# All attention in float32 on quarters of TensorE's array, causal half only, with the first weights decoded first

## The chip, the core and the metric

The kernel runs on one core of a Trainium2 chip. Its engines are TensorE (PE in the profile; PEld is its weight load), VectorE (DVE), ScalarE (ACT), GpSimd (POOL) and SyncE (SP), whose queue issues the transfers. The metric is device time in microseconds (us), lower is better.

## The reference

Decayed causal attention over batch 4, 8 heads, 768 positions, head size 64, then a feed-forward network (FFN) with a squared ReLU, on 3072 tokens of 512 features.

```python
for b in range(nb):                                   # blocks of 64 positions
    intra = einsum('bhic,bhjc->bhij', qb, kb) * Dmask     # lam**(i-j) where i >= j, else 0
    intra = einsum('bhij,bhjd->bhid', intra, vb)
    inter = einsum('bhid,bhde->bhie', qb * lam**(pos+1), kv_state)
    out[:, :, sl] = intra + inter
    kv_state = lam**64 * kv_state + einsum('bhsd,bhse->bhde', kb * lam**(63-pos), vb)
x = out as (tokens, heads * 64)
h = maximum(x @ w_in, 0)                              # w_in 512 x 2048, float64
return (h * h) @ w_out                                # w_out 2048 x 512, float64
```

q, k, v are float32, lam is one number per head; the weights arrive as float64.

## The kernel before

**Work units.** The kernel works on chunks of 128 positions, all eight heads; there are 24 chunks (4 batches of 6). Three chunks make a tile of 384 tokens, and there are 8 tiles. For each tile the attention writes x, transposed, as two parts: `xh`, rounded to the type float32r, and `xl`, the rest. The FFN runs over 16 feature blocks `f` of 128. One *step* is one tile and one `f`: 12 matmuls into `h` (L514: xh with the high weights `wih`, xl with `wih`, xh with the low weights `wil`), the squared ReLU split into `gh` and `gl` on ScalarE and VectorE (L528 to L535), and 9 matmuls (L520, L521, L523) that add to three output banks. There are 128 steps. From the third tile on, two steps are taken together. A full tile's output is copied out (L569) and stored (L570).

**Weights.** For each `f` there are two weight blocks, `w_in` and `w_out`. Each is loaded as 64-bit words into `st` (L277) and decoded to float32 in `m`: one operation on ScalarE (L278), four on VectorE (L279, L281, L283, L285). Then ScalarE rounds it to the high part (L287) and VectorE subtracts for the low part (L288). The blocks stay on the chip, and tiles 0 and 1 run through `f` as the weights come.

**Attention.** Each chunk is done in two units of four heads. With the decay taken apart, the scores are masked (not decayed), v is weighted by a table `wdec`, and the output is multiplied by a table `rdec`; the state of a batch and head is kept, multiplied by `lc` from chunk to chunk. The 12 units of the two first tiles and 4 of the third (the 8 chunks of `PLAIN`) are `unit_plain`: float32 matmuls, scores with 64 rows of the array per head (L318), state and values (L372, L375), the update of the state (L346). The other 16 chunks (32 units) are `unit_split`: q, k, v, the masked scores and the state are each cast to a high part and a low part (`ab`, `ka`, `vv`, `pp`, `ss`), and float32r matmuls over the full array take high and low parts together (scores L436, state L478, values L479); VectorE and ScalarE cast, subtract and add the parts (L412 to L497). Only the update (L456) is float32. Scores are computed for the full 128 x 128 square and then masked.

**What sets the order.** `Plan` holds all operations with an engine, a planned duration, a key, dependencies and buffers (`SLOTS` gives the number of each kind; `bank` is a PSUM bank). `Plan.order` places them one after another: on each engine, of those that can start within 0.05 us, the one with the lowest key. The result is one fixed order for each engine, and each engine then runs its instructions in that order. All loads are issued from SP's queue, which takes them in order, so a load that waits for its buffer holds back the loads behind it. Early in the program the plan puts in matmuls on zeros (`filler`, L240) where TensorE would have nothing to do. The buffers of `unit_split` take the place of those of the decoding and of `unit_plain` when these are done (`late`).

Of the kernel before, what the change touches and what calls it, by code (L numbers as in the profile page):

```python
# [9 lines left out]
F32 = mybir.dt.float32  # L10
# [16 lines left out]
NQ = NP // 2  # L27
PK = 1536
# [12 lines left out]
N_PLAIN = 8  # L41
PLAIN, SPLIT = CHUNKS[:N_PLAIN], CHUNKS[N_PLAIN:]
# [10 lines left out]
class Op:  # L53
    def __init__(self, eng, dur, key, fn, deps, bufs, after, lat, early):
        self.eng, self.dur, self.key, self.fn, self.deps, self.bufs, self.after, self.lat, self.early = (
            eng, dur, key, fn, deps, bufs, after, lat, early)
        self.start = self.end = None


class Plan:  # L60
    LAT = {"PE": 0.25, "ACT": 0.15, "DVE": 0.12, "POOL": 0.12, "SP": 2.0}
    PORT = ("DVE", "POOL")
# [7 lines left out]
    def op(self, eng, dur, key, fn, deps=(), bufs=(), after=(), lat=None, early=None):  # L70
        o = Op(eng, dur, key, fn, [d for d in deps if d is not None], list(bufs), [d for d in after if d is not None], lat or self.LAT[eng], early)
        for b in o.bufs:
            b.left += 1
        self.ops.append(o)
        return o

    def order(self, pe_slow, fill):
# [10 lines left out]
        done, filled, early = [], 0, sum(o.early is True for o in self.ops)  # L88
        while any(ready.values()):
            best = None  # L90
            for e, ops in ready.items():
                can = []
                for o in ops:
# [5 lines left out]
                    ok = o.early is not False or not early  # L99
# [15 lines left out]
            if o.eng == "PE" and t < fill:  # L115

                while free["PE"] + (long := FILL * (2.0 if free["PE"] < pe_slow else 1.0)) < t:
# [3 lines left out]
                    done.append(Op("PE", long, 0, lambda i=bank[1]: self.filler(i), [], [], [], 0, None))  # L121
# [16 lines left out]
            early -= o.early is True  # L138
# [14 lines left out]
EARLY = ("pnt", "diag0", "diag1", "st", "m")  # L153
LATE = ("pkt", "ab", "ka", "vv", "pp", "z", "zl", "ss0", "ss1")

FIRST, SLOW_STEP, LAG, BEGIN2, SECOND, STEP, PE_SLOW, FILL_END, FILL = 18.0, 6.5, 16, 9.0, 1.5, 4.8, 7.0, 45.0, 0.43
# [3 lines left out]
SPARE = 0.8  # L162

TWO, BOTH = 2, 9.0


@with_exitstack
def kernel(ctx: ExitStack, tc: tile.TileContext, pn, pk, lamx, w, out):
# [3 lines left out]
    phase = ExitStack()  # L172
    plan = Plan()
    for k, n in SLOTS.items():
# [4 lines left out]
        "bank": ([P, 512], F32), "h": ([P, 512], F32),  # L179
        "gh": ([P, N], F32R), "gl": ([P, N], F32R), "g": ([P, N], F32), "ob": ([P, DM], F32),  # L180
        "s1": ([P, 4, C], F32), "vd": ([P, 4, D], F32), "us": ([P, 2, D], F32), "xr": ([P, 2, C], F32),
        "st": ([P, DM], U64), "m": ([P, DM], F32), "pnt": ([P, 4, 2, P], F32), "diag0": ([P, 2, P], F32), "diag1": ([P, 2, P], F32),
        "pkt": ([P, PK], F32), "ab": ([P, 4, 2, C], F32R), "ka": ([P, 4, C], F32R), "vv": ([P, 4, 2, D], F32R),
        "pp": ([P, 4, 2, C], F32R), "z": ([P, 2, 2, C], F32), "zl": ([D, 2, 2, C], F32),
        "ss0": ([P, 2, 2, 2, D], F32R), "ss1": ([P, 2, 2, 2, D], F32R), "hold": ([P, 2, D], F32)}
# [6 lines left out]
    make(ps, ("bank", "h"))  # L192
    make(const, [k for k in SLOTS if k not in EARLY + LATE + ("bank", "h", "x")])

    tables = const.tile([P, 16], F32, name="tables")
    wdec, lc = tables[:, 0:H], tables[:, H:H + NP]
# [4 lines left out]
    flip, zero = tiles["g"][-1][:, 0:P], tiles["ob"][-1]  # L201
    lam, ej, ec = (tiles["g"][-1][:, P + 16 * i:P + 16 * i + n] for i, n in enumerate((H + NP, H, NP)))
    mask = const.tile([P, P], F32, name="mask")
# [4 lines left out]
    make(phase.enter_context(tc.tile_pool(name="early", bufs=1)), EARLY)  # L208

    def late():  # L210
        phase.close()
        make(ctx.enter_context(tc.tile_pool(name="late", bufs=1, reuse_waits="tile")), LATE)

        for k in ("ss0", "ss1"):
            for s in tiles[k]:
                nc.gpsimd.memset(s.bitcast(F32), 0.0)
# [4 lines left out]

    def start_tables():
        nc.sync.dma_start(out=lam, in_=lamx)
        nc.vector.memset(zero, 0.0)
        nc.gpsimd.iota(ej, pattern=[[0, H]], base=MID, channel_multiplier=-1, allow_small_or_imprecise_dtypes=True)
        nc.vector.memset(ec, float(C))

        nc.vector.memset(flip, 1.0)
        nc.vector.memset(mask, 1.0)
        nc.gpsimd.affine_select(out=flip, in_=flip, pattern=[[1, P]], compare_op=ALU.is_equal, fill=0.0, base=1 - P, channel_multiplier=1)  # L230
        nc.gpsimd.affine_select(out=mask, in_=mask, pattern=[[1, P]], compare_op=ALU.is_ge, fill=0.0, base=0, channel_multiplier=-1)

        for d in tiles["diag0"] + tiles["diag1"]:
            nc.gpsimd.memset(d, 0.0)

        nc.gpsimd.tensor_tensor(out=wdec, in0=lam[:, 0:H], in1=ej, op=ALU.pow)
        nc.gpsimd.tensor_tensor(out=lc, in0=lam[:, H:H + NP], in1=ec, op=ALU.pow)
# [6 lines left out]
    o_start = plan.op("POOL", 1.2, -99, start_tables, early=True)  # L244


    o_pow = plan.op("POOL", 3.0, -98, lambda: None, [o_start], early=True)
    wb, rps = Buf("m"), Buf("bank")

    def turned():  # L250
        for n in range(NP):
# [411 lines left out]
```

## Time and profile before

| | |
|---|---|
| time, median of 3 runs | 633.93 us (633.67 to 634.47) |
| span of the profiled execution, first to last instruction | 631.5 us (the page gives no other time of it; the median is 2.4 more) |
| TensorE busy | 624.0 us, 99% |
| VectorE, ScalarE, GpSimd busy | 476.5, 360.9, 5.9 us |
| transfers | 57.24 MB, mean 91 GB/s |
| instructions | 9583 |

A matmul's record includes the time in the array's pipeline, so records of matmuls overlap: what a matmul costs is read from the spacing of starts, not from its duration. In a row of the timeline stand the start, the time from the first start to the last end, the engine, the line, the operation, `out<-in`, the array shape (rows*columns), the streamed operand (partitions x columns) and, behind the x, the number of instructions. In a row of the windows stand the stretch, its length, then busy us and (x instructions) of PE, PEld, DVE, ACT and POOL, the granted clock of TensorE as a share of full speed, the share of the DMA engines that is busy, and GB/s.

### The profile page before, as it was taken

Reading aid. Unit: us, or ns where it says so; the run is one execution under the profiler, and the core shown is the slowest. Engines: PE = TensorE matmul, PEld = TensorE weight load, DVE = VectorE, ACT = ScalarE, POOL = GpSimd, SP = SyncE. Lnnn points to the kernel's source line nnn. Section 1 sums busy time; section 2 is a strip of 40 time slices with the busy share of each in tenths; the row PEclk is TensorE's granted clock in tenths of the full one; section 3 lists DMA queues with packets and bytes.
Section 4 is the critical chain, followed back from the end, with each engine's and each line's share of the span. In section 5 each row is a group of like instructions: output and inputs, shape, how many; then the busy total and the mean of one; then the engine's idle time right before and its main releaser. Section 6 shows DMA issues by size and latency. Waiting matters only on the chain.

```text
span 631.5 us, 9583 instructions
## 1 busy us (share of the span) xinstructions
PE 624.0 (99%) x3608; PEld 568.7 (90%) x3608; DVE 476.5 (75%) x1078; ACT 360.9 (57%) x841; POOL 5.9 (1%) x15
## 2 busy tenths in 40 slices
PE   9899999999999999999999999999999999999997
PEld 7798999888999999999999999999999999999996
DVE  5999999846767997598965999669994799733222
ACT  5887777656856574376744666455753657522221
POOL 2000000000000000000000000000000000000000
PEclk9999999999999999999999999999999999999999
DMA  8735556523221220321303222131210411000001
GB/s 299 269 106 186 176 173 195 200 81 121 101 81 52 70 101 0 102 101 50 101 1 102 100 70 81 51 101 50 101 51 0 150 51 51 1 32 20 0 1 50
DMA packets 15166, 57.24 MB, mean 91 GB/s; under 512 B 1808, under 2 KB 1808, under 8 KB 15120
## 3 DMA queue, kind: packets, MB, share of 16 engines
q1 hardware_dynamic: 15120, 56.64, 26.3%
q8 instruction: 28, 0.46, 0.3%
q14 instruction: 18, 0.15, 0.1%
HBM read 50.34 MB, written 6.29 MB: 90 GB/s over the span
## 4 chain that ended last, share of the span: by engine, by line
PE 96%; DVE 3%; ACT 1%; issue 0%
PE h L514 42%; PE bank L523 14%; PE bank L520 14%; PE bank L521 14%; PE bank L479 2%; PE bank L478 2%; PE bank L436 2%; PE bank L456 2%; PE bank L318 1%; PE bank L240 1%; PE bank L375 1%; DVE s L323 1%; ACT diag L362 0%; PE bank L372 0%; DVE xr L378 0%; PE bank L346 0%
## 5 line engine op out<-in xcount | busy, mean ns | idle before, releaser
L520 PE MATMUL bank<-woh,gh 128*128 128x512 f32 x384 | 150.3, 392 | 0.0
L521 PE MATMUL bank<-wol,gh 128*128 128x512 f32 x384 | 150.1, 391 | 0.0
L528 ACT ACTIVATE g<-h 128x384 f32<-128x384 f32 x128 | 62.8, 491 | 144.2 <-PE h L514 143.4
L514 PE MATMUL h<-xh,wih 128*128 128x384 f32 x512 | 111.9, 340 | 0.0
L514 PE MATMUL h<-xh,wil 128*128 128x384 f32 x512 | 109.6, 336 | 0.0
L514 PE MATMUL h<-xl,wih 128*128 128x384 f32 x512 | 109.6, 336 | 0.0
L534 DVE TENSOR_TENSOR g<-g 128x384 f32<-128x384 f32 x96 | 53.4, 556 | 68.2 <-ACT gh L533 68.1
L523 PE MATMUL bank<-woh,gl 128*128 128x512 f32 x384 | 100.6, 390 | 0.2 <-DVE gl L535 0.2
L514 PEld LDWEIGHTS h<-xh,wih 128*128 128x128 f32 x512 | 89.7, 188 | 5.2
L514 PEld LDWEIGHTS h<-xh,wil 128*128 128x128 f32 x512 | 90.6, 188 | 0.0
L514 PEld LDWEIGHTS h<-xl,wih 128*128 128x128 f32 x512 | 90.3, 188 | 0.0
L523 PEld LDWEIGHTS bank<-woh,gl 128*128 128x128 f32 x384 | 71.7, 188 | 15.0 <-DVE gl L535 0.4
L520 PEld LDWEIGHTS bank<-woh,gh 128*128 128x128 f32 x384 | 72.2, 188 | 13.2 <-issue 0.2
L521 PEld LDWEIGHTS bank<-wol,gh 128*128 128x128 f32 x384 | 72.2, 188 | 13.1
L535 DVE TENSOR_TENSOR gl<-g,gh 128x384 fp32r<-128x384 f32 x128 | 70.7, 553 | 6.6 <-ACT gh L531 3.5
L533 ACT ACTIVATE gh<-g 128x384 fp32r<-128x384 f32 x96 | 50.5, 526 | 31.8 <-PE bank L521 30.5
L486 DVE TENSOR_TENSOR z<-bank,z 128x256 f32<-128x256 f32 x64 | 27.0, 421 | 25.1 <-ACT z L485 25.0
L447 ACT CAST pp<-s 128x512 fp32r<-128x512 f32 x32 | 19.9, 622 | 24.5 <-DVE s L445 24.5
L479 PE MATMUL bank<-pp,vv 128*128 128x256 f32 x128 | 32.0, 283 | 0.0
L478 PE MATMUL bank<-ab,ss 128*128 128x256 f32 x128 | 31.8, 282 | 0.0
L491 DVE TENSOR_TENSOR xr<-z,zl 64x256 f32<-64x256 f32 x64 | 26.7, 417 | 2.7 <-ACT zl L487 1.0
L569 DVE COPY ob<-bank 128x512 f32<-128x512 f32 x15 | 10.3, 689 | 22.0 <-PE bank L523 21.6
(80 smaller groups left out, 792.0 us busy)
## 6 DMA issues: line engine op xcount, KB each, us to landing
pkt<-pk SPq DMA_DIRECT2D x32, 768.0 KB, 4.4
st<-w SPq DMA_DIRECT2D x32, 512.0 KB, 3.3
pnt<-pn SPq DMA_DIRECT2D x16, 512.0 KB, 4.9
out<-ob SPq DMA_DIRECT2D x23, 256.0 KB, 2.3
out<-z SPq DMA_DIRECT2D x1, 256.0 KB, 2.0
g<-lamx SPq DMA_DIRECT2D x1, 6.0 KB, 1.6
```

The source lines that it names most:

```text
L478: nc.tensor.matmul(y4[:, n], at(ss)[:, n, h].rearrange("p t d -> p (t d)"), at(ab)[:, i], start=n == 0, stop=False, skip_group_check=True)
L479: nc.tensor.matmul(y4[:, n], at(vv)[:, i].rearrange("p t d -> p (t d)"), at(pp)[:, i], start=False, stop=True, skip_group_check=True)
L486: zo.append(add("DVE", 0.36, 2, lambda h=h, part=part: nc.vector.tensor_tensor(out=at(z)[:, h], in0=part(0), in1=at(z)[:, h], op=ALU.add), ...
L491: nc.vector.tensor_tensor(out=at(xr)[half(h)], in0=at(z)[0:64, h], in1=at(zl)[:, h], op=ALU.add)
L514: nc.tensor.matmul(at(h)[:, 0:N], wt[:, cc, :], xt[:, cc, :], start=k == 0, stop=k == 3 * NCC - 1)
L520: nc.tensor.matmul(at(os_[j]), at(gh)[:, sl], woh[f], start=f == 0, stop=False)
L521: nc.tensor.matmul(at(os_[j]), at(gh)[:, sl], wol[f], start=False, stop=False)
L523: nc.tensor.matmul(at(os_[j]), at(gl)[:, sl], woh[f], start=False, stop=f == NF - 1)
L528: orr = plan.op("ACT", 0.45, key, lambda: nc.scalar.activation(at(g), at(h)[:, 0:N], AF.Relu), [o1], [h, g])
L533: ogh = plan.op("ACT", 0.47, key, lambda: nc.scalar.activation(at(gh), at(g), AF.Square), [orr], [g, gh])
L534: og = plan.op("DVE", 0.48, key, lambda: nc.vector.tensor_tensor(out=at(g), in0=at(g), in1=at(g), op=ALU.mult), [orr, ogh], [g])
L535: ogl = plan.op("DVE", 0.48, key, lambda: nc.vector.tensor_tensor(out=at(gl), in0=at(g), in1=at(gh), op=ALU.subtract), [og, ogh], [g, gh, gl])
```

## The change

All 24 chunks now take one path in float32, on whole chunks of eight heads, and `unit_split` with its casts is gone. The array is used as four quarters of 64 x 64. Keys are taken in two halves of 64 (`j`), and for the second half of the keys only the second half of the queries is computed (`C - j * TW` columns), so that scores and values leave out the quarter above the diagonal. The matmuls of four quarters stand in turn (`QUARTERS`), and those that share rows of the array write to one bank, the others to another.

The four first chunks (`unit_first`) multiply their scores by a table of mask times decay (`dm`), which is built at the start (`spread`, L252, L266, L268); their v needs no weighting for the values, and their output no `rdec`. The other chunks (`unit`) mask, and use `wdec` and `rdec` as before. From the third tile on, one operation on TensorE holds a chunk's scores (L344) and update (L350) and the state (L452) and values (L358) of the chunk before it (`turn_over`). The weighting of v is on ScalarE in the two first tiles (L368), on VectorE later. The plan's keys put the first `w_in` block ahead of the loads of q, k and v. All eight banks are of one kind now (`h` takes one of them, with a token `turn` so that at most two do), buffers `in` are shared by weights and attention, and nothing is exchanged late. The FFN's matmuls are the same (now L485, L491, L492, L494), the decode too (now L289 to L300).

```diff
-FIRST, ..., SECOND, ... = 18.0, ..., 1.5, ...
+FIRST, ..., SECOND, ... = 9.0, ..., 5.0, ...
+TW = C // 2
+SPAN = C + TW
+QUARTERS = ((0, 0), (1, 1), (0, 1), (1, 0))
+WEIGHTS0, WKEY1, WKEY2, KLATE, ULATE = -9.0, 7.0, 2.0, 6.0, 16.0
...
+    def scores(t, sc):
+        for e in range(2):
+            for j in range(2):
+                for r, v in QUARTERS:
+                    o_ = at(sc[r])[half(v), e * SPAN + j * C:e * SPAN + j * C + C - j * TW]
+                    nc.tensor.matmul(o_, k_(t, r, 2 * v + e, j), q_(t, r, 2 * v + e, j * TW), ...)
+    def update(kt, vd, u, col, start):
+        for e in range(2):
+            for j in range(2):
+                for v, r in QUARTERS:
+                    nc.tensor.matmul(
+                        at(u[v])[half(r), col + e * D:col + e * D + D], kt()[half(v), head(r, j, e)],
+                        heads(at(vd))[half(v), head(r, j, e)], ...)
+    def values(v_, s1, ys, start):
+        for r in range(R):
+            for j in range(2):
+                for v, e in QUARTERS:
+                    nc.tensor.matmul(
+                        at(ys[v])[half(e), (2 + r) * C + j * TW:(3 + r) * C], v_()[half(v), head(r, j, e)], at(s1[r])[half(v), e, j * C:j * C + C - j * TW], ...)
...
     # unit(), every chunk but the four first
+        def both():
+            for v in range(2):
+                for r, e in QUARTERS:
+                    nc.tensor.matmul(at(ys[r])[half(e), v * C:v * C + C], at(old)[half(r), 2 * v + e], q_(t, r, 2 * v + e), ...)
+            values(lambda: heads(at(vd)), s1, ys, False)
+        def back(o_y):
+            oc = [add("ACT", ..., nc.scalar.copy(x4(xr)[:, 2 * r:2 * r + 2], at(ys[r])[:, 0:2 * C]...)) for r in range(R)]
+            oa = [add("DVE", ..., nc.vector.tensor_tensor(out=by_v(x4(xr), v), in0=y_(ys, v), in1=by_v(x4(xr), v), op=ALU.add)) for v in range(2)]
+            xo = add("DVE", ..., nc.vector.tensor_tensor(out=x4(xr), in0=x4(xr), in1=rdec, op=ALU.mult))
+            oh = add("ACT", ..., nc.scalar.copy(at(x)[0][:, :, cs], x4(xr)))
+            ol = add("DVE", ..., nc.vector.tensor_tensor(out=at(x)[1][:, :, cs], in0=x4(xr), in1=at(x)[0][:, :, cs], op=ALU.subtract))
...
     # unit_first(), the four first chunks
+        so = [add("DVE", ..., nc.vector.tensor_tensor(out=at(s1[r]), in0=at(sc[r])..., in1=dm()[:, 2 * r:2 * r + 2], op=ALU.mult)) for r in range(R)]
...
-        ws.append((weights(f, 0, t - 7), weights(f, 1, t - 2)))
+        ws.append((weights(f, 0, t - WKEY1 if f else WEIGHTS0), weights(f, 1, t - WKEY2)))
...
+    def turn_over(u):
...
+        def run(before=pending[0][0]["values"].fn if pending else None):
+            if f:
+                f.fn()
+            if before:
+                before()
```

How the order moves is shown at three places. A row gives the line, the operation, `out<-in` (numbers are buffers), and the shape that is streamed; x is a count.

VectorE near the start. Before, the first operations are the weighted v (`vd`) and the masked scores (`s`) of units:

```order
L255 COPY m_181<-tables 128x512
L332 TENSOR_TENSOR vd_90<-pnt_170,tables 128x256
L323 TENSOR_TENSOR s_0_88<-bank_61,mask 128x2x128
L323 TENSOR_TENSOR s_0_88<-bank_62,mask 128x2x128
L323 TENSOR_TENSOR s_1_89<-bank_64,mask 128x2x128
L323 TENSOR_TENSOR s_1_89<-bank_65,mask 128x2x128
L332 TENSOR_TENSOR vd_90<-pnt_172,tables 128x256
L259 TENSOR_TENSOR rdec<-bank_61,g_77 128x512
```

Now the same place on VectorE holds the decode of the first weight block (`m_102` from `in_86`) and the decay table (`in_89`):

```order
L259 COPY m_101<-tables 128x512
L262 TENSOR_TENSOR tables<-tables,g_77 128x4
L291 TENSOR_SCALAR m_102<-m_102 128x512
L293 TENSOR_SCALAR m_102<-m_102 128x512
L295 SCALAR_TENSOR_TENSOR m_102<-in_86,m_102 128x512
L266 SCALAR_TENSOR_TENSOR in_89<-bank_61,tables,mask 128x128 x4
L297 SCALAR_TENSOR_TENSOR m_102<-in_86,m_102 128x512
L268 COPY in_89<-in_89 128x4x64
L391 TENSOR_TENSOR s_0_91<-bank_62,in_89 128x384
L391 TENSOR_TENSOR s_1_92<-bank_63,in_89 128x384
```

The first block's decode has moved ahead of all scores; before, it began behind those of the first units.

TensorE around the first step. Before, the scores (L318) of nine units, six of tile 0 and three of tile 1, stand ahead of the first FFN matmuls (L514), and what directly surrounds these is:

```order
L375 MATMUL bank_63<-s_1_89,vd_91 64x128 x4
L346 MATMUL bank_61<-vd_91,pnt_173 64x64 x4
L346 MATMUL bank_65<-vd_90,pnt_170 64x64 x4
L514 MATMUL h_67<-xh_96,wih_103 128x384 x4
L514 MATMUL h_67<-xl_97,wih_103 128x384 x4
L514 MATMUL h_67<-xh_96,wil_119 128x384 x4
L372 MATMUL bank_64<-pnt_170,diag_0_174 128x128 x2
```

Now, on the same engine, the first FFN matmuls (L485) stand between the scores and the values of tile 1's first chunk:

```order
L344 MATMUL bank_68<-in_87 64x64
L344 MATMUL bank_61<-in_87 64x64
L485 MATMUL bank_62<-xh_105,wih_112 128x384 x4
L485 MATMUL bank_62<-xl_106,wih_112 128x384 x4
L485 MATMUL bank_62<-xh_105,wil_128 128x384 x4
L358 MATMUL bank_63<-s_2_93,half_95 64x128
L358 MATMUL bank_64<-s_2_93,half_95 64x128
```

The step has moved ahead of most of tile 1's attention; three steps of tile 0, not one, now stand ahead of the first step of tile 1, and the updates of tile 0's chunks come behind their values.

TensorE in a later tile. Before, a unit's state and values (L478, L479) stand between steps, its scores and update elsewhere:

```order
L514 MATMUL h_68<-xh_96,wil_132 128x384 x4
L478 MATMUL bank_62<-ab_1554,ss_0_1561 128x256
L479 MATMUL bank_62<-pp_1557,vv_1556 128x256
L478 MATMUL bank_62<-ab_1554,ss_0_1561 128x256
L479 MATMUL bank_62<-pp_1557,vv_1556 128x256
L478 MATMUL bank_63<-ab_1554,ss_0_1561 128x256
L479 MATMUL bank_63<-pp_1557,vv_1556 128x256
L478 MATMUL bank_63<-ab_1554,ss_0_1561 128x256
L479 MATMUL bank_63<-pp_1557,vv_1556 128x256
L514 MATMUL h_67<-xh_96,wih_117 128x384 x4
```

Now a part of one chunk's stretch reads (the end of the update, the state, and the first values of the chunk before):

```order
L350 MATMUL bank_67<-half_99,in_89 64x64
L452 MATMUL bank_62<-in_87,hold_80 64x128
L452 MATMUL bank_61<-in_87,hold_80 64x128
L452 MATMUL bank_62<-in_87,hold_80 64x128
L452 MATMUL bank_61<-in_87,hold_80 64x128
L452 MATMUL bank_62<-in_87,hold_80 64x128
L452 MATMUL bank_61<-in_87,hold_80 64x128
L452 MATMUL bank_62<-in_87,hold_80 64x128
L452 MATMUL bank_61<-in_87,hold_80 64x128
L358 MATMUL bank_62<-s_0_91,half_96 64x128
L358 MATMUL bank_61<-s_0_91,half_96 64x128
```

The 16 scores, 16 update, 8 state and 16 value matmuls of a stretch stand in one piece, once a chunk, and move between two pairs of steps.

More of the change, by code (lines that the diff above doesn't have):

```diff
@@ L87, in order @@
         slots = {k: [(0.0, i) for i in range(n)] for k, n in self.slots.items()}
-        done, filled, early = [], 0, sum(o.early is True for o in self.ops)
+        done, filled = [], 0
         while any(ready.values()):
@@ L207 @@
     wol = [const.tile([P, DM], F32R, name=f"wol{f}") for f in range(NF)]
[L208 to L216, printed above, removed]
     def at(b):
         return tiles[b.kind][b.slot]
+    halves = [slice(h * TW, h * TW + TW) for h in range(2)]
     def start_tables():
@@ L308, in add, with unit_first @@
+    def unit_first(b, x, col, key):
+        t, tv, tk, vd, s1, sc, ys, u, new = (
+            Buf("in"), Buf("half"), Buf("half"), Buf("half"), [Buf("s1") for _ in range(R)], [Buf("bank") for _ in range(2)], [Buf("bank") for _ in range(2)],
+            [Buf("bank") for _ in range(2)], Buf("hold"))
         def add(eng, dur, dk, fn, deps, bufs, name=None):
-            o = plan.op(eng, dur, key + dk, fn, deps, bufs, early=True)
+            o = plan.op(eng, dur, key + dk, fn, deps, bufs)
             return in_turn(name, o) if name else o
-        load = add("SP", 1.7, -8, lambda: nc.sync.dma_start(out=at(t), in_=pn[PLAIN.index((b, c)), q]), [o_start, behind], [t], "load")
@@ L313, in unit_plain @@
-        sc = [Buf("bank"), Buf("bank")]
-        def scores():
-            for n in range(2):
-                for h in range(2):
-                    nc.tensor.matmul(at(sc[h])[:, n * C:n * C + C], at(t)[half(h), 0, n], at(t)[half(h), 1, n], start=True, stop=True)
-        o = add("PE", 0.66, 0, scores, [load], [t] + sc, "sc")
-        if (b, c, q) == (0, 0, 0):
-            o_turned.after.append(o)
-        so = [add("DVE", 0.36, 0, lambda h=h: nc.vector.tensor_tensor(
-            out=at(s1).rearrange("p (n h) i -> p n h i", h=2)[:, :, h], in0=at(sc[h])[:, 0:2 * C].rearrange("p (n i) -> p n i", n=2),
-            in1=mask.unsqueeze(1).broadcast_to([P, 2, C]), op=ALU.mult), [o], [sc[h], s1], f"s1{h}") for h in range(2)]
@@ L377, in unit_plain @@
-        o = add("PE", 1.25 if old else 0.8, 0.2, values, so + [o_vd] + ([old[1]] if old else []), [y, t, vd, s1, x] + ([old[0]] if old else []), "y")
-        o = add("DVE", 0.35, 0.2, lambda: nc.vector.tensor_tensor(
-            out=at(xr), in0=at(y)[:, 0:2 * C].rearrange("p (n i) -> p n i", n=2), in1=rdec[:, prs], op=ALU.mult), [o, o_rdec], [y, xr], "xr")
-        cs = slice(col, col + C)
-        oh = add("ACT", 0.33, 0.2, lambda: nc.scalar.copy(at(x)[0][:, prs, cs], at(xr)), [o], [xr, x])
@@ L502 @@
     last_mm, steps = {}, {}
     def ffn(ti, f, x, ready, wo, os_, key, held):
[L506 removed]
+        h, turn_, gh, gl, g = (Buf(k) for k in ("bank", "turn", "gh", "gl", "g"))
         last = ti == len(TILES) - 1 and f == NF - 1
@@ new lines, with attention @@
+            if ti < 2:
+                done_x[ti] += unit_first(b, xs[ti], j * C, key) if c == 0 else unit(b, c, xs[ti], j * C, key, 0.2, vd_act=True, alone=True)
+    def attention(ti):
+        for j, (b, c) in enumerate(TILES[ti]):
+            u = unit(b, c, xs[ti], j * C, begin[ti - 1] + (j - LEAD) * NF / NT * per[ti - 1], 4.0, steps[0, BEHIND] if ti == 2 else None)
+            u["last"] = begin[ti - 1] + (NT - LEAD) * NF / NT * per[ti - 1]
+            so = turn_over(u)
+            pending.append((u, so, done_x[ti]))
@@ L609 @@
     done = plan.order(PE_SLOW, FILL_END)
-    opened = False
-    n_early = sum(o.early is True for o in done)
     with tc.manual_schedule():
         for o in done:
-            if o.early is False and not opened:
-                assert n_early == 0, "an earlier buffer is still in use"
-                late()
-                opened = True
             o.fn()
-            n_early -= o.early is True
 def kernel(q, k, v, lam, moe_w_in, moe_w_out):
```

437 lines of the change are left out of this document (211 added, 226 removed), and 4 rows, old and new, of the table SLOTS.

## The prediction

> **What bounds the kernel now.** I read the page first, there the chain that ended last, by engine.
>
> ```profile
> PE 96%; DVE 3%; ACT 1%; issue 0%
> ```
>
> TensorE (PE) carries 96% of the chain, so the time is a sum of what TensorE must do, plus a start in which it lacks work. I split it so. An FFN step (one feature block of one tile: the 12 matmuls of L514 and the 9 of L520, L521 and L523) is priced from the chain in order of time, in the stretch near the end where nothing else runs; the start and the end come from TensorE's timeline and the windows.
>
> ```profile
> 549.42 4.16 PE h L514 x24
> ...
> 615.45 4.16 PE h L514 x24
> 23.95 0.96 PE L514 MATMUL h<-xh,wih 128*128 128x384 f32 x4
> ...
> 36.93 0.85 PE L514 MATMUL h<-xh,wih 128*128 128x384 f32 x4
> 600.00:631.50 31.50, 27.78 (x138) 24.59 (x137) 8.09 (x14) 6.68 (x13) 0.00 (x0) 0.97 0.07 25
> ```
>
> Eight pairs of steps lie between 549.42 and 615.45, so a step is 66.03/16 = 4.127 us, and all 128 take 528.2. By TensorE's order one step was done at 36.93, and the attention of tiles 0 and 1. TensorE's last 27.78 us end at 627.8, and 3.7 follow (the last copy and transfer). Between 36.93 and 627.8 are 590.9 us; 127 steps take 524.1; the other 66.7 are the attention of the 18 chunks of tiles 2 to 7, **3.7 us a chunk**. These two terms, the start and the 66.7, are what the change can move.
>
> **Removed: the split attention.** One split unit (half a chunk) stands in TensorE's timeline:
>
> ```profile
> 204.45 0.64 PE L436 MATMUL bank<-ab,ka 128*128 128x256 f32 x4
> 204.92 0.40 PE L520 MATMUL bank<-woh,gh 128*128 128x512 f32 x1
> ...
> 211.11 0.28 PE L478 MATMUL bank<-ab,ss 128*128 128x256 f32 x1
> ...
> 212.06 0.61 PE L456 MATMUL bank<-vd,pkt 128*128 128x128 f32 x4
> 212.43 0.94 PE L514 MATMUL h<-xh,wih 128*128 128x384 f32 x4
> 213.21 0.86 PE L514 MATMUL h<-xl,wih 128*128 128x384 f32 x4
> ```
>
> Scores 0.47; values and state 0.95; the update with the four L514 behind it 1.15, less 0.69 for four L514 alone (131.52 to 132.21, below), 0.46: 1.88 us. 32 such units, 8 without an update, are 56.5; the four old-style units of tile 2 are the other 10. VectorE and ScalarE lose the casts and subtractions as well, which I cost at nothing: they run beside TensorE's matmuls (VectorE is 3% of the chain, and that in the start).
>
> **Added: quarter matmuls.** A float32 matmul appears as two instructions in the trace (L318: 64 in the code, 128 shown). A chunk now has 56 matmuls, so 112 instructions: 48 that stream 128 columns and 64 that stream 64, and 32 of the latter fall away in the four last chunks, which have no update. The trace has no quarters, but it has halves: L375 and L346 use 64 columns of the array two at a time, L318 64 rows two at a time.
>
> ```profile
> L346 PE MATMUL bank<-vd,pnt x128: 219/222/270, 6.3 to 143.2; 128*64 128x64 f32 x128
> L318 PE MATMUL bank<-pnt x128: 272/272/373, 5.7 to 146.1; 64*128 64x128 f32 x128
> 27.26 1.16 PE L318 MATMUL bank<-pnt 64*128 64x128 f32 x16
> ...
> 129.28 0.86 PE L514 MATMUL h<-xh,wil 128*128 128x384 f32 x4
> 130.07 0.72 PE L318 MATMUL bank<-pnt 64*128 64x128 f32 x8
> 130.71 0.97 PE L514 MATMUL h<-xh,wih 128*128 128x384 f32 x4
> 131.52 0.86 PE L514 MATMUL h<-xl,wih 128*128 128x384 f32 x4
> 132.21 0.86 PE L514 MATMUL h<-xh,wil 128*128 128x384 f32 x4
> 132.91 0.60 PE L372 MATMUL bank<-pnt,diag 128*128 128x128 f32 x4
> 133.44 0.66 PE L375 MATMUL bank<-s,vd 128*64 128x128 f32 x8
> 133.93 0.63 PE L346 MATMUL bank<-vd,pnt 128*64 128x64 f32 x16
> 134.49 0.50 PE L520 MATMUL bank<-woh,gh 128*128 128x512 f32 x1
> 134.83 0.40 PE L521 MATMUL bank<-wol,gh 128*128 128x512 f32 x1
> ```
>
> The spacing of starts is (length of the group less one duration) over the count less one. L346, 64 columns in column halves: (0.63-0.222)/15 = 27 ns. L318, row halves, 128 columns: (1.16-0.272)/15 = 59 ns. With L318's duration for the other two that stream 128 columns, L375, column halves, is (0.66-0.272)/7 = 55 ns, and the full array (L372) (0.60-0.272)/3 = 109. So both kinds of halves run two at a time, and weight loads stay hidden. The product of both halvings would be 27.6 ns for 128 columns and 13.6 for 64. The bounds: below by the product; above, nothing better than the halves (55 and 27). I take the product, because each halving alone gave its full factor of two within a tenth, and the quarters are issued so that four neighbours never share a quarter. A chunk is then 48 x 27.6 + 64 x 13.6 = 2.20 us.
>
> A change of the array's split costs too. L318 between L514: 129.28 + 0.69 to 131.52 is 1.55 us; less 0.69 for the four L514 and 8 x 59 ns leaves 0.38 for going in and out. From 132.91 to 134.83: 1.92, less 0.23 for L520, 4 x 109, 8 x 55 and 16 x 27 ns, leaves 0.38 again. The new order gathers a chunk's scores and update with the values of the chunk before into one stretch, so it pays 0.38 once a chunk, 19 times. Attention after the start: 18 x (2.20+0.38) - 4 x 32 x 13.6 ns + 0.38 = **45.0 us instead of 66.7**. What waits there: the values need scores that VectorE masked a chunk earlier, some 25 us before, so no wait; the stretch holds four banks beside three output banks, and a later matmul of L485 needs one of them back, a mask of 0.5 us and a state add against 2.1 us of L485. I cost that at nothing; without this cover it is about 1 us a chunk.
>
> **The start.** It is VectorE that sets it: busy 8.98 and 9.91 of the 10 us from 10 and from 20.
>
> ```profile
> 0.00:10.00 10.00, 8.48 (x64) 6.66 (x66) 4.31 (x13) 3.42 (x9) 4.48 (x13) 1.00 0.78 282
> 10.00:20.00 10.00, 9.23 (x118) 7.04 (x118) 8.98 (x25) 9.39 (x31) 0.00 (x0) 1.00 0.93 331
> 20.00:30.00 10.00, 8.69 (x110) 7.58 (x112) 9.91 (x28) 9.00 (x28) 0.00 (x0) 1.00 0.77 254
> ```
>
> and, from the timelines of VectorE and ScalarE,
>
> ```profile
> 5.22 0.42 DVE L332 TENSOR_TENSOR vd<-pnt,tables 128x256 f32<-128x256 f32 x1
> ...
> 38.67 0.76 DVE L281 TENSOR_SCALAR m<-m 128x512 uint32<-128x512 uint32 x2
> 39.35 1.28 DVE L283 SCALAR_TENSOR_TENSOR m<-st,m 128x512 uint32<-128x512 uint32 x2
> 6.53 1.28 ACT L329 ACT_TABLE_LOAD   x1 [6.53 <-DMA pnt<-pn]
> 15.07 0.67 ACT L278 ACTIVATE m<-st 128x512 f32<-128x512 f32 x1
> ```
>
> Successive VectorE starts give the price of each: 0.34 (two L281 in 0.76, one lasts 0.42) and 0.59 (L283), so a weight of two light and three heavy operations is 2.45 us. The first block now lands first: SP's queue issues it ahead of the loads of q, k and v, which puts the first scores back by one load of 0.5 MB, 1.8 us at the 282 GB/s of the first window; all that tile 0 needs, 2.8 MB, is in by 10 us, so transfers don't set the end. A first load is in by 5.22 at the latest; then the table load 1.28 and the first |w| 0.67 on ScalarE give VectorE work at 7.0. Behind it, to the last operation of tile 0, stand the decode (2.45), the decay table (about 1.3 with its copy), three chunks of scores (6 of about 0.5, by 384 columns instead of L323's 256) and the subtractions and rdec (8 of 0.34): 9.5 us. With about 1 for the third chunk's values and casts, tile 0 is ready at **17.4, where 23.95 stood**. Between there and tile 1's last operation VectorE now has 5 weights and half a sixth (13.5 us), 6 masks (3.0), 3 low parts (1.4), and the state and output operations of three chunks (6.9): 24.8, so 42.2, and with 1.3 of waits on ScalarE **43.5**. But three steps are done by then, by TensorE's order, and not one. Before, TensorE at 43.5 had done 1 + (43.5-36.93)/4.127 = 2.6. So the early 6.5 us come to 0.4 step, 1.7 us, since the same VectorE must decode more weights ahead of tile 1. Bounds for 43.5: 40 (no waits, masks at L323's price) and 50 (ScalarE, whose eight scalings a chunk stand ahead of casts, adds a wait to each chunk).
>
> **Sum.** 43.5 + 125 x 4.127 (515.9) + 45.0 + 3.7 = 608.1 for the span. The median of the runs, 633.93, is 2.4 above the span, so 610.5.
>
> **Rivals.** *A floor per instruction.* No start spacing in the trace is under 27 ns, however short the matmul, so the 64-column ones may stay at 27.2: a chunk is 48 x 27.6 + 64 x 27.2 = 3.07, attention 18 x 3.45 - 4 x 0.87 + 0.38 = 59.0, and the time 624.5. For it: L346 sits exactly there. Against it: 27 is also just what two halves of the array give. The Trainium skill, page "TensorE: Matmul & The Clock Gate", section "Wait — 56ns, not 53.3ns?", says that start-to-start never drops below about 25 ns; by its figure the 64-column instructions would be an estimated 25 ns and the time about 622. The same page's Part 3 lets packed tiles start about 4 ns apart, which would remove this floor; no run so far shows either.
>
> *Quarters overlap only like halves* (row and column halving don't multiply, or weight loads surface). At 55 and 27 ns a chunk is 4.40 + 0.38, attention 82.9, the time 648: slower. It turns at attention 68.4, that is (68.4-7.2)/1888 = 32 ns an instruction on average, against 20 by the product and 27 by the floor. Against it: L318 keeps its pace with 128-column weights, twice what is loaded now.
>
> *The start goes late.* Tile 1 at 50 instead of 43.5 gives 617: SP waits in turn for the shared input buffers, and behind a waiting load all later loads wait.
>
> **How the numbers follow.** The product, with the start as worked out: 0.62; the floor: 0.20; the late start alone: 0.09; quarters like halves: 0.07; no visible change: 0.02. The range runs from 603 (tile 1 at 40, a change of split at half its price: 610.5-3.5-3.6) to 625, the floor's time, and leaves about 0.15 out. Faster by over 0.2% (about what a measurement of this kernel can tell from none) 0.91, same 0.02, slower 0.07.
>
> **What will show it.** L344, L350, L452 and L358 in the timeline of TensorE: 2.6 us a chunk with its edges by the product, 3.4 by the floor, 4.8 by halves; spacing of L350 under 20 ns for the product, at 25 to 27 for the floor. The first L485 near 17.4, tile 1's first near 43.5. L485 to L494 again at 4.13 a step; if a step grows, a bank came back late. Wrong, too, if TensorE shows idle time between 45 and 120, where weights arrive in the order of a plan.

## The result, and the profile after

The changed kernel takes **611.65 us** (median of 4 runs, 611.45 to 611.9), the kernel before beside it on the same chip 634.16 (633.67 to 634.47): a ratio of **0.9644**, 95% interval 0.9631 to 0.9658. The forecast was 610.5. The profiled execution has a span of 610.2 us.

The page of the profile after:

```profile
span 610.2 us, 12175 instructions
PE 603.4 (99%) x5268; PEld 544.0 (89%) x5268; DVE 310.0 (51%) x623; ACT 224.8 (37%) x477; POOL 4.6 (1%) x14
PE 96%; DMA 2%; DVE 1%; ACT 0%; issue 0%; SPq 0%; DVEq 0%
```

TensorE is still the bound, with the same share of the chain. VectorE lost 166.5 us of work and ScalarE 136.1, but they had held only 3% and 1% of the chain before, so the 22 us came for the most part from TensorE's own rows. One chunk's stretch and what follows it, in TensorE's timeline after:

```profile
204.67 0.90 PE L344 MATMUL bank<-in 64*64 64x128 f32 x32
205.39 0.65 PE L350 MATMUL bank<-half,in 64*64 64x64 f32 x32
205.86 0.62 PE L452 MATMUL bank<-in,hold 64*64 64x128 f32 x16
206.29 0.85 PE L358 MATMUL bank<-s,half 64*64 64x128 f32 x32
207.07 0.50 PE L491 MATMUL bank<-woh,gh 128*128 128x512 f32 x1
...
211.29 0.86 PE L485 MATMUL bank<-xh,wih 128*128 128x384 f32 x4
...
238.66 0.86 PE L485 MATMUL bank<-xh,wih 128*128 128x384 f32 x4
```

All 112 instructions of a chunk start between 204.67 and 207.07. From 211.29 to 238.66, 27.37 us, TensorE does six FFN steps and one such stretch. Steps stand in the chain of waits after, near the end where nothing else runs:

```profile
552.37 4.16 PE bank L485 x24
...
593.64 4.16 PE bank L485 x24
```

That is 41.27 us for ten steps, 4.127 each, as before. So the stretch with both its edges costs 27.37 - 24.76 = 2.61 us, where a chunk cost 3.7. The spacing inside it needs one duration, from the view of L350 by its line (minimum, median, maximum in ns):

```profile
L350 PE MATMUL bank<-half,in x512: 218/218/254, 25.3 to 481.2; 64*64 64x64 f32 x171
```

On average L350 starts every (0.65-0.218)/31 = **13.9 ns**. The product of both halvings had said 13.6, the floor 25 to 27. The single starts are not evenly spaced. Cut off at 205.44 and at 205.50, the timeline has

```profile
205.39 0.24 PE L350 MATMUL bank<-half,in 64*64 64x64 f32 x4
205.39 0.30 PE L350 MATMUL bank<-half,in 64*64 64x64 f32 x8
```

Four records that last 0.218 us each fit into 0.24, so their starts, one for each quarter in the order of the code, lie 7 ns apart; the next four follow (0.65-0.24)/7 = 59 ns after them. In the trace before, two halves had done the same: its timeline, cut off at 133.95, has

```profile
133.93 0.23 PE L346 MATMUL bank<-vd,pnt 128*64 128x64 f32 x2
```

that is, two records of 0.222 us that start some 10 ns apart.

The two ends of the program, from TensorE's timeline after:

```profile
16.78 0.96 PE L485 MATMUL bank<-xh,wih 128*128 128x384 f32 x4
...
44.27 0.86 PE L485 MATMUL bank<-xh,wih 128*128 128x384 f32 x4
```

and from its windows:

```profile
45.00:120.00 75.00, 75.00 (x440) 68.28 (x439) 74.70 (x155) 53.92 (x103) 0.00 (x0) 1.00 0.56 181
600.00:610.20 10.20, 5.97 (x27) 4.62 (x25) 2.50 (x4) 1.11 (x2) 0.00 (x0) 1.00 0.21 77
```

Tile 0's first step is at 16.78, tile 1's first at 44.27 with three steps done, TensorE has no idle time from 45 to 120 (75.00 of 75.00), and its last record ends at 605.97, 4.2 before the end of the span.

The difference of the two spans, 631.5 - 610.2 = 21.3 us, then splits so. The attention after the start takes 610.2 - 44.27 - 125 x 4.127 - 4.2 = 45.8 us instead of 66.7: 20.9. The start: before, TensorE at 44.27 had done 1 + (44.27-36.93)/4.127 = 2.78 steps, now 3: 0.22 step, 0.9 us. The end is 0.5 longer.

### The profile page after: what moved, and what is told of

The parts are those of the page before. It is cut to its first block, busy times and chain, and to the rows that moved or that the text cites. A ratio compares the mean times of both kernels' runs of the same rounds, so it can differ in the third digit from the quotient of the medians.

```text
span 610.2 us, 12175 instructions
## 1 busy us (share of the span) xinstructions
PE 603.4 (99%) x5268; PEld 544.0 (89%) x5268; DVE 310.0 (51%) x623; ACT 224.8 (37%) x477; POOL 4.6 (1%) x14
## 4 chain that ended last, share of the span: by engine, by line
PE 96%; DMA 2%; DVE 1%; ACT 0%; issue 0%; SPq 0%; DVEq 0%
PE bank L485 44%; PE bank L491 15%; PE bank L492 14%; PE bank L494 14%; PE bank L344 3%; PE bank L358 3%; DMA in<-w 2%; PE bank L452 2%; PE bank L350 1%; PE bank L230 1%; DVE in L266 0%; ACT m L290 0%; DVE xl L461 0%; DVE m L540 0%; DVE m L295 0%
## 5 line engine op out<-in xcount | busy, mean ns | idle before, releaser
L491 PE MATMUL bank<-woh,gh 128*128 128x512 f32 x384 | 151.7, 395 | 0.1
L492 PE MATMUL bank<-wol,gh 128*128 128x512 f32 x384 | 149.9, 390 | 0.0
L499 ACT ACTIVATE g<-bank 128x384 f32<-128x384 f32 x128 | 62.8, 491 | 191.2 <-PE bank L485 190.7
L485 PE MATMUL bank<-xh,wih 128*128 128x384 f32 x512 | 110.5, 338 | 0.0
L485 PE MATMUL bank<-xh,wil 128*128 128x384 f32 x512 | 109.6, 336 | 0.0
L485 PE MATMUL bank<-xl,wih 128*128 128x384 f32 x512 | 109.5, 336 | 0.0
L494 PE MATMUL bank<-woh,gl 128*128 128x512 f32 x384 | 100.6, 390 | 0.0
L485 PEld LDWEIGHTS bank<-xh,wih 128*128 128x128 f32 x512 | 91.1, 188 | 4.6
L485 PEld LDWEIGHTS bank<-xh,wil 128*128 128x128 f32 x512 | 90.6, 188 | 0.0
L485 PEld LDWEIGHTS bank<-xl,wih 128*128 128x128 f32 x512 | 90.4, 188 | 0.0
L491 PEld LDWEIGHTS bank<-woh,gh 128*128 128x128 f32 x384 | 72.1, 188 | 14.6 <-ACT gh L502 0.6
L494 PEld LDWEIGHTS bank<-woh,gl 128*128 128x128 f32 x384 | 71.9, 188 | 14.7
L492 PEld LDWEIGHTS bank<-wol,gh 128*128 128x128 f32 x384 | 72.1, 188 | 12.9
L290 ACT ACTIVATE m<-in 128x512 f32<-128x512 f32 x32 | 21.5, 675 | 14.2 <-DVE wol L300 6.2
L344 PEld LDWEIGHTS bank<-in 64*64 64x64 f32 x768 | 18.5, 133 | 7.6 <-issue 6.9
L437 DVE TENSOR_TENSOR s<-bank,mask 128x384 f32<-128x384 f32 x40 | 20.6, 552 | 9.1 <-PE bank L350 8.2
L297 DVE SCALAR_TENSOR_TENSOR m<-in,m 128x512 uint32<-128x512 uint32 x32 | 22.1, 690 | 0.0
```

Source lines behind the costliest of these rows:

```text
L290: o = add("ACT", 0.55, lambda: nc.scalar.activation(at(m), words(1).bitcast(F32), AF.Abs), [o], [st, m])
L297: o = add("DVE", 0.6, lambda: nc.vector.scalar_tensor_tensor(out=bits(), in0=words(0), scalar=29, in1=bits(), op0=ALU.logical_shift_right, ...
L344: nc.tensor.matmul(o_, k_(t, r, 2 * v + e, j), q_(t, r, 2 * v + e, j * TW), start=e == j == 0, stop=True, skip_group_check=True)
L437: so = [add("DVE", 0.45, 0.2, lambda r=r: nc.vector.tensor_tensor(out=at(s1[r]), in0=at(sc[r])[:, 0:2 * SPAN].rearrange("p (e i) -> p e i" ...
L485: nc.tensor.matmul(at(h)[:, 0:N], wt[:, cc, :], xt[:, cc, :], start=k == 0, stop=k == 3 * NCC - 1)
L491: nc.tensor.matmul(at(os_[j]), at(gh)[:, sl], woh[f], start=f == 0, stop=False)
```

## The experiments

All times stand against the kernel before on the same chip (633.7 to 633.84 in the three groups). The change itself, run again:

> The change itself, again, as the measure for the three runs on the start beside it: 611.7 us, ratio 0.964 to before, tile 1's first step at about 44.3 us, the first step at 16.8.

It took 611.85 (610.67 to 612.19, four runs), ratio 0.9652 (0.964 to 0.9665); in its profile the first step is at 17.60, tile 1's first at 44.20. Single runs of one kernel thus differ by up to 1.5 us, and the first step moves by 0.8 between two profiled executions.

### Do four quarters have to stand in turn?

The loops are turned so that all matmuls of one quarter stand in a row, in each of the four groups:

```diff
-        for e in range(2):
-            for j in range(2):
-                for r, v in QUARTERS:
+        for r, v in QUARTERS:
+            for e in range(2):
+                for j in range(2):
```

> The change, with the loops of scores, update, state and values turned so that all matmuls of one quarter of the array come one after another, and only then those of the next. If the product of both halvings comes from four neighbours that run in four different quarters, this loses it: 128-column instructions at 109 ns and 64-column ones at 54, so a chunk's stretch goes from 2.6 us to about 48 x 109 + 64 x 54 ns = 8.7, plus 0.4; over 18 chunks and the start 105 to 125 us more, about 725 us. If order among the quarters is free (the queue looks ahead far enough), a stretch stays near 2.6 us and the time near 612. If there is a pace per instruction that hides it, anything between, with one spacing for all four lines.

It took 673.03 us (one run): order matters, but less than with one quarter at a time. Its stretch in TensorE's timeline:

```profile
231.23 1.82 PE L344 MATMUL bank<-in 64*64 64x128 f32 x29
232.78 0.27 PE L350 MATMUL bank<-half,in 64*64 64x64 f32 x1
...
233.06 0.22 PE L344 MATMUL bank<-in 64*64 64x64 f32 x1
233.07 1.08 PE L350 MATMUL bank<-half,in 64*64 64x64 f32 x25
...
236.35 0.50 PE L491 MATMUL bank<-woh,gh 128*128 128x512 f32 x1
...
261.33 1.82 PE L344 MATMUL bank<-in 64*64 64x128 f32 x29
```

From its first start to the first L491 are 5.12 us instead of 2.40. The next stretch starts 30.10 us later, which is six steps and 5.34 us, so 0.2 us of the edges lie outside these bounds, as in the change (2.61 against 2.40). With 0.30 of edges taken off (measured below), an instruction costs (5.34-0.30)/112 = 45 ns on average here, and 21 in the change. One quarter at a time would be 4 x 2.20 us/112 = 79, by the prediction's terms. And L350's first instructions, in the first quarter of their group, start while L344's last ones, in another quarter, have not yet started. So the starts aren't in program order across quarters: an instruction whose quarter is free goes ahead of one whose quarter is busy, over some distance. That each engine runs its instructions in the fixed order, as the description of the kernel before has it, thus does not hold for TensorE's starts. The stretches after the start hold 1888 instructions, 16.9 times 112, and carry 16.9 x 2.72 = 46 us of the 61.2 lost against the change. The twelve stretches of the start, read from the two timelines in the same way, take 31.9 us instead of 16.4, which is the rest.

Two quarters in turn, then the other two (the loops' order again, nothing else):

```diff
+TWO_BY_TWO = [(a, j, p) for n in range(0, 4, 2) for a in range(2) for j in range(2) for p in QUARTERS[n:n + 2]]
...
-        for e in range(2):
-            for j in range(2):
-                for r, v in QUARTERS:
+        for e, j, (r, v) in TWO_BY_TWO:
```

> The change with only two quarters in turn: first all matmuls of quarters (0,0) and (1,1), one and the other in turn, then all of (0,1) and (1,0). Next neighbours share neither rows nor columns, but a stretch of 16 (state: 8) instructions runs on two quarters. If each quarter takes 109 and 54 ns an instruction for itself and two run at a time: 55 and 27 ns, a stretch of about 4.7 us instead of 2.6, some 650 us. But the run with one quarter at a time took 43 ns an instruction where 78 were expected, and its trace shows the next line's first quarter starting before the last one of the line before ends; by this look-ahead (rival) the next pair starts early here too, the spacing is 24 to 27 ns on average, and the time 612 to 625 us.

625.61 us (one run), 0.6 beyond the range that the look-ahead gave, and far below the 650 of two at a time. In its timeline (L343 the scores, L347 the update) the same mixing is seen:

```profile
209.85 1.06 PE L343 MATMUL bank<-in 64*64 64x128 f32 x26
210.64 0.27 PE L347 MATMUL bank<-half,in 64*64 64x64 f32 x2
210.74 0.28 PE L343 MATMUL bank<-in 64*64 64x128 f32 x2
...
212.88 0.50 PE L485 MATMUL bank<-woh,gh 128*128 128x512 f32 x1
...
237.89 1.06 PE L343 MATMUL bank<-in 64*64 64x128 f32 x26
```

From one stretch to the next are 28.04 us, six steps and 3.28 us: (3.28-0.30)/112 = 27 ns an instruction. Runs of 8 instructions in one quarter (4 for the state) cost 45 ns each, runs of 16 in two quarters 27, four quarters in turn 21. Last, the order of the four in a turn, so that neighbours share rows of the array:

```diff
-QUARTERS = ((0, 0), (1, 1), (0, 1), (1, 0))
+QUARTERS = ((0, 0), (0, 1), (1, 0), (1, 1))
```

> The change, with QUARTERS in the order (0,0), (0,1), (1,0), (1,1): four neighbours are still four quarters, but next neighbours now share the rows (scores, update, state, values alike), where in the change they share neither rows nor columns. If only the set of four matters: 2.6 us a stretch and 611.7 us, no difference. If a weight load overlaps only with a neighbour in other rows (rival), each second load shows: some 10 to 25 ns for every second instruction, 0.6 to 1.4 us a chunk, 622 to 640 us.

611.23 us (610.82 to 611.63), ratio 0.9647 (0.9633 to 0.9662): no difference from the change. What counts is that all four stand near one another, not which two are neighbours.

### What is the causal half worth?

```diff
-  o_ = at(sc[r])[half(v), e * SPAN + j * C:e * SPAN + j * C + C - j * TW]
-  nc.tensor.matmul(o_, k_(t, r, 2 * v + e, j), q_(t, r, 2 * v + e, j * TW), ...)
+  o_ = at(sc[r])[half(v), e * SPAN + j * C:e * SPAN + j * C + C]
+  nc.tensor.matmul(o_, k_(t, r, 2 * v + e, j), q_(t, r, 2 * v + e), ...)
...
-  at(ys[v])[half(e), (2 + r) * C + j * TW:(3 + r) * C], ..., at(s1[r])[half(v), e, j * C:j * C + C - j * TW],
+  at(ys[v])[half(e), (2 + r) * C:(3 + r) * C], ..., at(s1[r])[half(v), e, j * TW:j * TW + C],
```

> The change without its causal half: the second half of the keys is multiplied with all 128 queries in scores and values, so the 32 instructions of a chunk that streamed 64 columns there stream 128 (what they compute beyond the diagonal lands on columns of the neighbour, so the output is not the reference's; masks and all else are as in the change). By the product each costs 13.8 ns more: 0.44 us a chunk, 18 chunks after the start, 7.9 us, 619.6 us. If short instructions pay a floor of about 27 ns anyhow, nothing changes: 611.7.

619.73 us (619.52 to 620.06), ratio 0.9782 (0.9767 to 0.9796), as computed from 27.6 and 13.6 ns; 7.9 to 8.1 more than the change (611.85 and 611.65). In TensorE's timeline the scores lie 0.92 us ahead of the update, where the change has 0.72:

```profile
206.84 1.10 PE L344 MATMUL bank<-in 64*64 64x128 f32 x32
207.76 0.64 PE L350 MATMUL bank<-half,in 64*64 64x64 f32 x32
```

### What does a change of the array's split cost?

The units run with `alone=True`, so that scores with update and state with values are two operations, placed apart; TensorE's order has 47 stretches on quarters instead of 31 (one pair still lies together, so 16 more and not the 17 of the expectation).

```diff
-            u = unit(b, c, xs[ti], j * C, ..., steps[0, BEHIND] if ti == 2 else None)
...
-            so = turn_over(u)
-            pending.append((u, so, done_x[ti]))
+            done_x[ti] += unit(b, c, xs[ti], j * C, ..., steps[0, BEHIND] if ti == 2 else None, alone=True)
```

> The change with the scores and update of a chunk and the state and values of the one before as two operations in different places, not one stretch: 17 more entries into the quartered array and back. By the 0.38 us that going in and out cost in the trace before: 6.5 us more, 618.1 us. If the edges are hidden (the array drains while the next weights load): within 1 us of 611.7. If waits for the masks come in as well, more than 620, with idle time of TensorE in front of L452 or L358.

616.54 us (616.11 to 616.72), ratio 0.9729 (0.9713 to 0.9745). From its timeline:

```profile
206.59 0.90 PE L344 MATMUL bank<-in 64*64 64x128 f32 x32
...
207.89 0.97 PE L485 MATMUL bank<-xh,wih 128*128 128x384 f32 x4
...
216.34 0.67 PE L452 MATMUL bank<-in,hold 64*64 64x128 f32 x16
...
217.61 0.97 PE L485 MATMUL bank<-xh,wih 128*128 128x384 f32 x4
```

Against the change it loses 4.8 us (the span 615.0 - 610.2, the medians 4.7 to 4.9), or 4.8/16 = 0.30 us for each further way in and out, rather than 0.38. The mechanism is as forecast. Part of the edge is seen: four L485 take 0.97 behind quarters, 0.86 behind L494.

### Is the start worth anything?

Three kernels: the change with its first weight block at the key it would have by the rule for the others; the change with no decay table; and the kernel before with only its first block moved ahead of q, k and v.

```diff
-        ws.append((weights(f, 0, t - WKEY1 if f else WEIGHTS0), weights(f, 1, t - WKEY2)))
+        ws.append((weights(f, 0, t - WKEY1), weights(f, 1, t - WKEY2)))
```

> The change with the first weight block's load and decode at the key of the others, behind the loads of the first two chunks. The prediction's account (the start is worth steps done by the time tile 1 is ready, and VectorE has the same work in either order): the first step comes 1 to 2 us later, tile 1's first step within 1 us of 44.3, and the time within 1 us of 611.7. Rival (the early first step is worth its own gain of 6 to 7 us over before): 2 us or more lost, with the loss equal to the delay of the first step.

```diff
-    o = plan.op("PE", 1.0, -12, spread, [o_wb], [wb, dps])
-    o_dm = [... nc.vector.scalar_tensor_tensor(out=dm()[:, h, 0:C], ...) ... for h in range(NS)]
-    o_dm = [... nc.vector.tensor_copy(dm()[:, :, C:SPAN], dm()[:, :, 0:TW]) ...]
...
-            in1=dm()[:, 2 * r:2 * r + 2], op=ALU.mult), ...
+            in1=mask.unsqueeze(1).broadcast_to([P, 2, SPAN]), op=ALU.mult), ...
```

> The change without the decay table: the first chunks' scores are multiplied by the mask alone, and the table's 16 matmuls and 6 VectorE operations (1.4 us) and its buffer fall away (the decay of the four first chunks is left out). If VectorE sets the start, tile 1 is ready 1.4 us earlier and the time is 610.3. If the waits for weight transfers in turn set it, the table is hidden behind them and the time stays within 0.5 us of 611.7, or falls by more only because a buffer is free.

```diff
 # the kernel before
-        ws.append((weights(f, 0, t - 7), weights(f, 1, t - 2)))
+        ws.append((weights(f, 0, t - 7 if f else -9.0), weights(f, 1, t - 2)))
```

> The kernel before with one part of the change alone: the first weight block's load ahead of the loads of the attention. By the prediction's account VectorE's work ahead of tile 1 is the same, so the first step comes earlier than 24.0 us but the time stays within 0.5 us of 634. Rival: the earlier first step is gained in full, 2 to 5 us, 629 to 632.

| kernel | us | ratio | tile 0's first step, tile 1's first |
|---|---|---|---|
| change | 611.85 | 0.9652 (0.964 to 0.9665) | 17.60, 44.20 |
| first block late | 611.71 (611.1 to 612.72) | 0.9655 (0.9643 to 0.9668) | 17.99, 45.42 |
| no table | 612.08 (610.22 to 613.18) | 0.9656 (0.9641 to 0.9672) | 16.13, 42.71 |
| before, first block ahead | 634.64 | 1.0014 (1.0005 to 1.0022) | 26.55, 38.84 |

None gains anything that the medians show; the last loses 0.14%, 0.64 us above the forecast 634 where 0.5 was allowed. With the first block late, the first step came only 0.4 us later, not 1 to 2, so this run can hardly tell the prediction's account from its rival; tile 1's first step came 1.2 later, a little outside the 1 us that was forecast. In the profile without the table, tile 1's first step comes 1.5 us earlier and the span is 608.5, as forecast, but that was the quickest of its runs, and the median is not below the change's: the 1.4 us of VectorE is not confirmed. Ahead of q, k and v alone, the kernel before does not even start earlier (26.55 against 23.95), so the premise of both theories for that run failed; why was not followed further.

### Two more tries on the start and the decode

The 13 filler matmuls that the plan puts in after its first 8 us are left out (they compute on zeros):

```diff
-..., PE_SLOW, FILL_END, FILL = ..., 7.0, 45.0, 0.43
+..., PE_SLOW, FILL_END, FILL = ..., 7.0, 8.0, 0.43
```

> The change without the matmuls on zeros after the first ten instructions (13 of 18 matmuls fall away, 26 instructions). They stand in the fixed order of TensorE ahead of real work: 6.2 us of them are on the chain that ends at 45 us. If that work could start earlier, up to 1 us is gained (tile 1's last operation on VectorE ends at 44.4, so no more); if they only fill waits, the time stays within 0.5 us of 611.8; if the granted clock falls in the gaps, matmuls of the start get slower and it is above 613.

613.5 us (611.67 to 614.14), ratio 0.9667 (0.965 to 0.9684): 1.7 more than the change by the medians, with intervals that overlap. The windows of this kernel:

```profile
10.00:20.00 10.00, 7.77 (x170) 7.04 (x171) 7.82 (x19) 8.81 (x33) 0.00 (x0) 0.83 0.95 312
40.00:50.00 10.00, 8.53 (x63) 7.67 (x64) 9.63 (x23) 4.77 (x10) 0.00 (x0) 0.83 0.49 159
```

and a row of its timeline:

```profile
17.59 1.65 PE L485 MATMUL bank<-xh,wih 128*128 128x384 f32 x4
```

With TensorE busy 7.77 and 8.53 of 10 us the granted clock is 0.83, a mean: in windows from 16 to 17 us and from 44 to 46 it is 0.50. Four L485 take 1.65 where they take 0.96 in the change, whose clock is 1.00 there. The busy share alone doesn't tell, since the kernel before has 1.00 with 8.69 of 10 (20 to 30 us). TensorE's longest idle times near these two places, where the change has fillers, are 1.34 us (up to 16.10) and 1.69 (up to 41.47). It is not so in every run: the three runs with a mean clock of 0.993 or 0.994 took 613.5 to 614.14 us, and the two with 0.997 and 1.0 took 611.67 and 611.73, as long as the change. So the loss goes with the clock, and without the fillers the clock falls in some runs.

VectorE is busy 74.70 of 75 us from 45 to 120 in the change. The low part of the weights (L300) is moved to GpSimd for all feature blocks but the first:

```diff
-        ol = add("DVE", 0.6, lambda: nc.vector.tensor_tensor(out=lo, in0=at(m), in1=hi, op=ALU.subtract), ...)
+        ol = add("POOL" if f else "DVE", 1.2 if f else 0.6, lambda: (nc.gpsimd if f else nc.vector).tensor_tensor(out=lo, in0=at(m), in1=hi, op=ALU.subtract), ...)
```

> The change with the low part of each decoded weight block but the first's subtracted on GpSimd instead of VectorE. If VectorE's work sets when tile 1 is ready, four to five subtractions of 0.6 us leave it: tile 1's first step 2 to 3 us earlier, 609 to 610 us. If the loads that wait for buffers set it (rival), it stays within 0.7 us of 611.8. If GpSimd is slow here or slows VectorE, weights come late: more than 613, with idle time of TensorE before 120 us.

637.85 us (637.15 to 638.75), ratio 1.0065 (1.0051 to 1.0078): slower than the kernel before. GpSimd's timeline in this kernel (its spans are rough in this profile),

```profile
84.34 1.45 POOL L300 TENSOR_TENSOR wol<-m,woh 128x512 fp32r<-128x512 f32 x1 [2.22 <-ACT woh L299]
87.41 1.47 POOL L300 TENSOR_TENSOR wil<-m,wih 128x512 fp32r<-128x512 f32 x1 [1.61 <-ACT wih L299]
```

VectorE's,

```profile
84.59 1.49 DVE L291 TENSOR_SCALAR m<-m 128x512 f32<-128x512 f32 x1
86.00 0.68 DVE L297 SCALAR_TENSOR_TENSOR m<-in,m 128x512 uint32<-128x512 uint32 x1
...
87.78 1.65 DVE L297 SCALAR_TENSOR_TENSOR m<-in,m 128x512 uint32<-128x512 uint32 x1
```

and a window of it:

```profile
80.00:100.00 20.00, 16.46 (x72) 14.58 (x71) 18.01 (x28) 11.66 (x22) 8.36 (x6) 0.83 0.47 160
```

L297 takes 0.68 with GpSimd idle, and 1.65 when it starts under a subtraction of GpSimd that ends at 88.88: nearly all of the 1.10 that the subtraction still has to go is added to it. L291, 0.42 in the change, is held to 1.49 in the same way, with 1.20 to go. The Trainium skill, page "SBUF — State Buffer", section "SBUF: two separate sides", says that the port pair which the two engines share is an exclusive lock for a whole instruction; the rows agree. The decode falls behind, TensorE is busy 16.46 of 20 us, and its clock falls too. VectorE itself gains nothing: 30 operations of 0.69 us have left it, and by the profile's page it is busy 322.1 us where the change has 310.0.

## Why the prediction was right

**The product holds.** "A chunk is then 2.20 us" plus 0.38 made 2.58; 2.61 was measured. Its two terms were off by a little, in opposite directions: the way in and out costs 0.30 by the experiment, which leaves 2.31 for the 112 instructions, 20.6 ns each instead of 19.6. Most of that is in the way the halves were read: the average over starts that come together makes them a little cheap. Four L350 every 59 ns are 14.7 ns each, not 13.6, and 64 times the difference is 0.07 of the 0.11 us. The reason "neighbours never share a quarter" was right in what it asked of the code, and the loops turned show it (673.03); the order of the pairs is of no account.

**The rivals.** The floor is excluded by 13.9 ns. Its premise, "No start spacing in the trace is under 27 ns", was a misreading of the trace before: 27 is the average over pairs of L346, a pair every (0.63-0.23)/7 = 57 ns, whose two starts lie some 10 ns apart. That trace alone spoke against the floor, and the prediction gave it 0.20. The Trainium skill's rule of about 25 ns from start to start, page "TensorE: Matmul & The Clock Gate", section "Wait — 56ns, not 53.3ns?", does not hold here for neighbours in different quarters: the measurement decides. Its Part 3, with small steps between packed tiles, allows what is seen, 7 ns. Quarters like halves is excluded by the same row, but its warning was worth something: two quarters in turn at 27 ns and one at 45 lie on both sides of the 32 ns at which the kernel would turn slower, and the run at 45 was slower. The late start did not come: 44.27, not 50.

**The gathering** was costed rightly in kind and 0.08 us too dear for each change of the split. Of the attention's 20.9 us, about 8 are the causal half and 4.8 the gathering, each measured by taking it away. The other 8 or so are left to the quarters themselves against the split matmuls; that is a remainder, not a measurement.

**The start** was forecast to be worth 1.7 us, and gave 0.9; the first step at 16.78 for 17.4, tile 1's at 44.27 for 43.5. The 0.9 is read from profiled executions; no run isolates it. Two details were wrong. The table load does not stand behind the first landing; ScalarE's timeline after:

```profile
0.80 1.28 ACT L290 ACT_TABLE_LOAD   x1 [0.80 <-PEq L642]
5.41 0.66 ACT L290 ACTIVATE m<-in 128x512 f32<-128x512 f32 x1 [3.33 <-DMA in<-w]
```

so VectorE's decode could begin at 6.11 instead of 7.0. The first step came 0.6 early here, but 0.2 late (17.60) when the change was run again, so this doesn't show in it. And a weight load stands on the chain of waits later, between 28 and 38 us:

```profile
28.81 0.67 PE bank L452 x16
...
29.49 6.42 DMA in<-w
...
35.94 0.02 ACT m L290
...
36.51 0.62 ACT xh L460
...
37.15 0.69 DVE xl L461
...
38.10 0.75 PE bank L452 x13
```

The load is released at 29.49, behind TensorE's state matmuls (L452), which read a buffer of the kind `in`, and lands at 35.91; ScalarE takes it (L290) ahead of the cast of x (L460), which tile 1 needs. That is the kind of wait that the rival of the late start had named, with 6.5 us for tile 1. It doesn't make the 0.8, though. When the change was run again, the chain of waits went through TensorE's own rows from 31.10 on, with no transfer in it,

```profile
31.10 0.50 PE bank L491
...
44.36 1.73 PE bank L485 x10
```

and tile 1's first step still stood at 44.20. "It is VectorE that sets it" holds at the last place before tile 1. Without the fillers, TensorE waits there for VectorE (L457):

```profile
41.47 0.69 PE L350 MATMUL bank<-half,half 64*64 64x64 f32 x30 [1.69 <-DVE half L457]
```

In the change eight filler instructions stand in that gap, and L350 starts at 41.48. So the fillers hide a wait for VectorE from the chain. Which of the terms in the forecast of 43.5 was 0.8 too small stays open.

**Errors that cancelled.** Against the sum: start +0.8, attention +0.8, end +0.5, together 610.2 for 608.1; but only 1.45 us lay between span and median where 2.4 were taken from before. In every run of these two kernels the time is 1.7 to 1.8 above the span of the same run (611.9 and 610.2, say); the 2.4 held about 0.7 by which the profiled execution before was quicker than the median. So 611.65 against 610.5 is closer than the span's terms were, and that is luck.

## What to carry to other kernels

When small matmuls use tiles of the array, write them so that all tiles come up within a few instructions: which tiles are neighbours made no difference here, while runs of 8 instructions in one tile cost 45 ns each instead of 21. Gather them, since each way from the full array to quarters and back cost 0.30 us, and count the steps of the next stage that are done by a given time, not the time at which the first one starts: 7.2 us of earlier first step was worth 0.9 us. Before work is moved to GpSimd to relieve VectorE, look at which of VectorE's operations will run beside it. Before a mean spacing of starts is taken for a floor, look at single starts: here the mean hid that tiles start together.

## What the runs showed of the hardware that was not expected

- TensorE starts instructions of different quarters out of program order: with one quarter at a time in the code an instruction costs 45 ns, not the 79 of the prediction's terms, and L350's first starts at 232.78 lie ahead of L344's last at 233.06.
- Matmuls in different tiles start 7 ns apart, and a quarter takes its next one (64 columns) 59 ns after the last: 13.9 ns is an average of these.
- A subtraction on GpSimd (1.45 us for 128 x 512) holds back VectorE operations that need 0.42 or 0.68 us alone, nearly until it is done; moving 30 subtractions there cost 26 us in all (637.85 against 611.85).
- Without 13 matmuls on zeros in the start, the granted clock fell to 0.50 at two places there in the profiled execution, with no idle time of TensorE over 1.69 us near them, and four L485 took 1.65 us instead of 0.96.
